# Block 3 of a fused attention and feed-forward kernel in the layout of the other blocks, with another order of units

## The chip, the cores and the metric

The kernel runs on one core of a Trainium2 chip. The metric is the device time of one execution in microseconds (us), the median of several runs. One execution of each kernel is profiled. The profile knows these engines: PE (TensorE, matmuls), PEld (its weight loads), DVE (VectorE), ACT (ScalarE), POOL (GpSimd) and SP (SyncE, which issues DMAs).

## The reference, cut to what matters

```python
xn = layernorm(x)                                   # x: 2048 rows of 640, bf16
q = (xn @ wq).reshape(1, 2048, 32, 192).transpose(0, 2, 1, 3)
k, v = the last 512 rows of each head's cache       # 32 heads, 192 wide
p = softmax(q @ k.T * 192 ** -0.5)
s = (p @ v, heads side by side) @ wo                # 2048 x 640
g = silu((silu(xn @ w_gate) * (xn @ w_up)) @ w_down)  # 2048 x 640
return x + s * g
```

## The kernel before: the parts that matter

The kernel treats the 2048 rows as four blocks of 512, and the 32 heads as 16 pairs. After the feed-forward part (which yields g) come 16 pairs of heads. For each pair and block there are query, score, product (`pv`) and output-projection units; the output projection of every pair is summed in SBUF, the on-chip working memory (`s_m`, `s_t`, `s_o`).

The projection has 640 columns, and no matmul of this kernel writes more than 512. Blocks 0 to 2 split them into 512 row-major columns (`s_m`: rows on partitions) and 128 transposed ones (`s_t`: columns on partitions, all 512 rows of the block in one matmul). Block 3 (`MB`) keeps all 640 row-major, as two halves of 320 (`s_o`). A row tile of a block is 128 of its 512 rows:

```python
HD, MB, MC = D // 2, NB - 1, D - P          # 320, block 3, 512

def wo_units(i):                            # units of one block in a stretch
    ...
    if b == MB:
        return [unit([(qt, cols) for cols in HALVES]) for qt in range(4)]
    return [unit([(2 * h + k, MAIN) for k in range(2)]) for h in range(2)] + [[rest]]
```

A unit's matmuls contract over 64 rows; two of them, on the upper and the lower half of the array, run side by side. In the first turn the two halves write two banks of PSUM (the memory that takes the matmuls' results), in the second turn they change banks. (Where the prediction speaks of row tiles and PSUM banks together, it means these halves of the array.) So that no two row halves ever write one bank together, a tiny GpSimd memset (`turn_t`) waits for the last matmul of the first turn, and the first matmul of the second turn waits for it:

```python
def wo_turn(st, i, tiles, turn):
    ps = st["sc"]
    for j in range(3):
        for n, r in enumerate((lo, hi)):    # rows 0..63, 64..127 of the array
            k = n ^ turn
            qt, cols = tiles[k]
            m = nc.tensor.matmul(
                ps[:, k, 0 : cols.stop - cols.start], OTs[i][r, 3 * qt + j, :],
                pairs[i // NB]["wo"][r, j, cols], ...)
            after(m, st)                    # wait for the memset of the turn before
    if turn == 0:
        turned(m, st)                       # nc.gpsimd.memset(turn_t) after this matmul

def rest():                                 # the transposed 128 columns: a bank for each half
    sc = sc_tile()
    for n, r in enumerate((lo, hi)):
        wo_rest(sc[:, n, :], i, r)
    for n in range(2):
        add_sum(pr + n, s_t[:, b, :], sc[:, n, :])
```

The order in which the units of one pair reach TensorE is written out. A digit is the block, a and b are the two halves of its product, w to z its output-projection units (of the block two earlier), and the last digit is the turn:

```python
LATER = """0a0 0b0 0y0 0x0 0a1 0x1 0w0 0b1 0w1 1x0 1a0 1x1 1b0 1w0 1a1 1w1 1z0 1b1 1z1 1y0 2b0 1y1
    2y0 2b1 2x0 2a0 2x1 3w0 2a1 3w1 2w0 3a0 2w1 3b0 3a1 3y0 3x0 3b1 3x1"""
```

In this text a stretch is one such sequence, about 23.6 us. Thirteen of them, for pairs 1 to 13, run block 3's units. The score and projection units share two PSUM tiles (`sc_tile`), queries and products share two others (`mm_tile`).

The softmax here doesn't subtract the row's maximum and nothing guards it: scores larger than these inputs give would overflow.

Of the kernel before, what the change touches and what calls it, by code (L numbers as in the profile page):

```python
# [15 lines left out]
def kernel(  # L16
# [13 lines left out]
    nc = tc.nc  # L30
# [20 lines left out]
    HD = D // 2  # L51
    MB = NB - 1
# [31 lines left out]
    g_m = res.tile([P, 4 * MB, MC], bf, name="g_m")  # L84
    g_t = res.tile([P, MB, 512], bf, name="g_t")
    g_o = res.tile([P, 4, D], bf, name="g_o")
    xT = res.tile([P, MB, 512], bf, name="xT")

# [82 lines left out]
    with ExitStack() as fctx:  # L171
# [131 lines left out]
        def ffn_down(b, u):  # L303


            dn = mm_tile()[:, 0, :]
            if b == MB:
                ti, n = divmod(u, 2)
                cols = slice(n * HD, (n + 1) * HD)
                dn, to = dn[:, 0:HD], g_o[:, ti, cols]  # L310
            elif u < 4:
                ti, cols = u, slice(0, MC)
                to = g_m[:, 4 * b + u, :]
            else:
                to = g_t[:, b, :]
            for f in range(NF):
                if b < MB and u == 4:
                    at, by = wd_sb[:, f, MC:D], hTs[b][:, f, :]
                else:
                    at, by = hTs[b][:, f, ti * P : (ti + 1) * P], wd_sb[:, f, cols]  # L320
                nc.tensor.matmul(dn, at, by, start=(f == 0), stop=(f == NF - 1))  # L321
            nc.scalar.activation(to, dn, ACT.Silu)
# [66 lines left out]
        for b in range(NB):  # L389
# [4 lines left out]
            for f in range(NF):  # L394
# [13 lines left out]
                if b < MB and f >= 8:  # L408
# [19 lines left out]
        for u in range(8):  # L428
            ffn_down(NB - 1, u)
            if u in (1, 3, 5):  # L430
                q_full(0, u // 2)
# [9 lines left out]
    s_m = sapool.tile([P, 4 * MB, MC], f32, name="s_m")  # L441
    s_t = sapool.tile([P, MB, 512], f32, name="s_t")
    s_o = sapool.tile([P, 4, D], f32, name="s_o")
# [114 lines left out]
    def load_xb(b):  # L558

        xbs[b] = finp.tile([P, 4, D], bf, name="x_b", bufs=NB)  # L560
        n = MC if b < MB else D
        nc.sync.dma_start(
            out=xbs[b][:, :, 0:n],
            in_=x2[b * 512 : (b + 1) * 512, 0:n].rearrange("(t p) d -> p t d", p=P),
        )

    def rows(b, qts):

        if b == MB:
            return s_o[:, qts, :], g_o[:, qts, :]  # L570
# [22 lines left out]
    HALVES = [slice(n * HD, (n + 1) * HD) for n in range(2)]  # L593
# [18 lines left out]
    def wo_turn(st, i, tiles, turn):  # L612

        ps = st["sc"]
        for j in range(3):
            for n, r in enumerate((lo, hi)):
                k = n ^ turn
                qt, cols = tiles[k]
                m = nc.tensor.matmul(  # L619
                    ps[:, k, 0 : cols.stop - cols.start], OTs[i][r, 3 * qt + j, :],  # L620
                    pairs[i // NB]["wo"][r, j, cols],
# [12 lines left out]
    def sum_rows(i, qts, sc):  # L634
        pr, b = divmod(i, NB)
        to, g = rows(b, qts)
        if b == MB:
            to = to.rearrange("p t (n d) -> p (t n) d", n=2)
            sc = sc[:, :, 0:HD]
# [15 lines left out]
    def add_x(b, qts=None):  # L655
        if qts is None:
            to, x = s_t[:, b, :], xT[:, b, :]
        else:
            to, x = rows(b, qts)[0], xbs[b][:, qts, 0 : MC if b < MB else D]
        nc.gpsimd.tensor_tensor(to, to, x, ALU.add)  # L660

    def wo_units(i):
# [4 lines left out]
        def unit(tiles):  # L667
            st, qts = {}, slice(tiles[0][0], tiles[1][0] + 1)

            def first():  # L670
                st["sc"] = sc_tile()
                wo_turn(st, i, tiles, 0)

            def second():
                wo_turn(st, i, tiles, 1)
                sum_rows(i, qts, st["sc"][:, :, :])
# [10 lines left out]
        if b == MB:  # L687
            return [unit([(qt, cols) for cols in HALVES]) for qt in range(4)]
        return [unit([(2 * h + k, MAIN) for k in range(2)]) for h in range(2)] + [[rest]]

    def wo_full(i, q2):

        pr, b = divmod(i, NB)
        if b == MB:
            units = [[(qt, cols) for cols in HALVES] for qt in (2 * q2, 2 * q2 + 1)]
        else:
            units = [[(2 * q2 + k, MAIN) for k in range(2)]]
        for tiles in units:
            sc, qts = sc_tile(), slice(tiles[0][0], tiles[1][0] + 1)
            for k, (qt, cols) in enumerate(tiles):  # L700
                wo_cols(sc[:, k, 0 : cols.stop - cols.start], i, qt, cols)
# [181 lines left out]
```

## Time and profile before

| | kernel before |
|---|---|
| device time, median | 921.71 us (921.47 to 921.82, 3 runs) |
| span of the profiled run | 919.5 us |
| TensorE busy, share of its chain | 99%, 99% |
| VectorE, ScalarE, GpSimd busy | 64%, 52%, 10% |

The prediction below shows the page's shares, the timeline and the last microseconds. What it does not show are the groups of instructions that the change replaces. In this view each line is: source line, engine, operation, out<-in, shapes and count | busy us, mean ns of one | idle time of the engine before them. These are from the view of groups by shape of the kernel before:

```profile
L619 PE MATMUL sc<-wo_p,OT_b 64*128 64x512 bf16 x984 | 128.1, 376 | 0.0
...
L632 DVE TENSOR_TENSOR s_m<-s_m,sc 128x1024 f32<-128x1024 f32 x82 | 100.2, 1222 | 48.7 <-PE sc L619 42.7 <-PE sc L579 5.9
...
L619 PE MATMUL sc<-wo_p,OT_b 64*128 64x320 bf16 x624 | 56.3, 296 | 0.0
L632 DVE TENSOR_TENSOR s_t<-s_t,sc 128x512 f32<-128x512 f32 x82 | 56.2, 685 | 18.0 <-PE sc L587 16.6
...
L632 DVE TENSOR_TENSOR s_o<-s_o,sc 128x640 f32<-128x640 f32 x52 | 42.6, 820 | 16.0 <-PE sc L619 14.8 <-PE sc L579 1.1
```

The 624 matmuls of 320 columns are block 3: 13 stretches of 48. The zero in the last field says that TensorE never sat idle before one of them. A mean of 376 ns for 512 columns is not what a matmul costs in a stream: the matmuls overlap in the pipeline, their ends are modelled, and their starts lie closer. The cost has to be read from start to start in the timeline.

### The profile page before, as it was taken

The numbers are of one execution on the slowest core, as the hardware profiler recorded it, in microseconds if no ns is written. First come the engines' busy times: TensorE is split into PE (matmuls) and PEld (weight loads), VectorE is DVE, ScalarE is ACT, GpSimd is POOL, SyncE is SP. The second block draws the span as 40 slices with busy tenths as digits, with TensorE's granted clock in tenths as the row PEclk, the third lists the DMA queues.
The fourth block names the chain that finished last, engine by engine and source line by source line (L and its number), as shares of the span: only waits on it lengthen the run. The fifth ranks groups of instructions, "written<-read, shape, count | busy, mean of one in ns | idle before, by whom it ended". The sixth has DMA issues, their size and how long they took to land.

```text
span 919.5 us, 23759 instructions
## 1 busy us (share of the span) xinstructions
PE 914.1 (99%) x10193; PEld 565.6 (62%) x10193; DVE 592.2 (64%) x842; ACT 474.3 (52%) x843; POOL 90.2 (10%) x298
## 2 busy tenths in 40 slices
PE   9999999999999999999999999999999999999998
PEld 6444445565757575757575757576666666666665
DVE  6443421467676767777777777676767676767656
ACT  4222222657464646565656555655555555556461
POOL 0000000000000000000000000000000000002977
PEclk9999999999999999999999999999999999999999
DMA  9312520045453425243534353435353434333526
GB/s 311 67 35 63 95 73 1 1 75 113 54 112 53 111 47 112 54 104 59 104 58 109 58 109 57 107 48 101 68 100 58 92 75 80 86 71 108 126 45 169
DMA packets 246969, 77.45 MB, mean 84 GB/s; under 512 B 227792, under 2 KB 246864, under 8 KB 246864
## 3 DMA queue, kind: packets, MB, share of 16 engines
q1 hardware_dynamic: 245376, 74.23, 39.2%
q8 instruction: 80, 1.31, 0.6%
q10 hardware_dynamic: 1488, 1.70, 0.6%
q14 instruction: 25, 0.20, 0.1%
HBM read 39.06 MB, written 2.62 MB: 45 GB/s over the span
## 4 chain that ended last, share of the span: by engine, by line
PE 99%; DVE 0%; POOLq 0%; POOL 0%; issue 0%; ACT 0%; DVEq 0%
PE mm L460 22%; PE sc L474 18%; PE sc L619 16%; PE mm L499 16%; PE sc L282 11%; PE mm L321 6%; PE sc L587 3%; PE sc L579 2%; PE mm L551 2%; PE mm L579 1%; PE gu L230 1%; PE gu L282 0%; PE mm L330 0%; PE sc L551 0%; PE sc L499 0%; PE mm L474 0%
## 5 line engine op out<-in xcount | busy, mean ns | idle before, releaser
L478 ACT ACTIVATE p_t<-sc 128x1024 bf16<-128x1024 f32 x254 | 252.9, 1022 | 120.6 <-PE sc L474 120.6
L465 DVE TENSOR_REDUCE qT<-mm 128x512 bf16<-128x1024 f32 x189 | 231.0, 1222 | 99.2 <-PE mm L460 96.7
L529 ACT ACTIVATE O_b<-mm,r 128x192 bf16<-128x192 f32 x486 | 164.6, 421 | 184.0 <-issue 138.4
L460 PE MATMUL mm<-xnT,wq_p 64*128 64x512 bf16 x1890 | 237.5, 376 | 0.0
L474 PE MATMUL sc<-qT,khat 64*128 64x512 bf16 x1524 | 198.0, 376 | 0.0
L619 PE MATMUL sc<-wo_p,OT_b 64*128 64x512 bf16 (+1 forms) x1608 | 182.1, 345 | 0.0
L499 PE MATMUL mm<-V_p,p_t 64*128 64x193 bf16 x3520 | 181.4, 242 | 0.0
L499 PEld LDWEIGHTS <-p_t 64*128 64x128 bf16 x3584 | 160.9, 93 | 28.8
L460 PEld LDWEIGHTS <-wq_p 64*128 64x128 bf16 x1890 | 105.0, 94 | 98.7 <-issue 0.7
L474 PEld LDWEIGHTS <-khat 64*128 64x128 bf16 x1536 | 85.3, 94 | 80.4 <-DVE s_t L632 0.3
L632 DVE TENSOR_TENSOR s_m<-s_m,sc 128x1024 f32<-128x1024 f32 x82 | 100.2, 1222 | 48.7 <-PE sc L619 42.7
L619 PEld LDWEIGHTS <-OT_b 64*128 64x128 bf16 x1608 | 85.8, 94 | 37.3 <-issue 0.3
L605 POOL MEMSET turn_t<- 128x1 f32 x246 | 24.1, 98 | 698.0 <-PE mm L499 494.7
L290 DVE TENSOR_TENSOR hT<-sc,sg 128x512 bf16<-128x512 f32 x46 | 31.7, 691 | 81.6 <-ACT sg L289 81.6
L632 DVE TENSOR_TENSOR s_t<-s_t,sc 128x512 f32<-128x512 f32 x82 | 56.2, 685 | 18.0 <-PE sc L587 16.6
L289 ACT ACTIVATE sg<-sc 128x512 bf16<-128x512 f32 x46 | 27.3, 596 | 69.8 <-PE sc L282 69.8
L282 PE MATMUL sc<-xnT,wg_sb 128*128 128x512 bf16 (+1 forms) x260 | 60.2, 354 | 0.3 <-ACT xnT L350 0.3
L282 PE MATMUL sc<-xnT,wu_sb 128*128 128x512 bf16 (+1 forms) x260 | 60.2, 354 | 0.0
L632 DVE TENSOR_TENSOR s_o<-s_o,sc 128x640 f32<-128x640 f32 x52 | 42.6, 820 | 16.0 <-PE sc L619 14.8
L321 PE MATMUL mm<-wd_sb,hT 128*128 128x512 bf16 (+1 forms) x240 | 46.7, 347 | 0.0
L518 DVE RECIPROCAL r<-mm 128x4 f32<-128x4 f32 x124 | 22.5, 182 | 37.3 <-PE mm L499 28.4
L282 PEld LDWEIGHTS <-wu_sb 128*128 128x128 bf16 x285 | 27.1, 98 | 27.1 <-issue 0.4
(95 smaller groups left out, 460.8 us busy)
## 6 DMA issues: line engine op xcount, KB each, us to landing
wo_p<-in_A_wo_dram SPq DMA_DIRECT2D x16, 480.0 KB, 4.6
K_p<-in_A_k_cache_dram SPq DMA_DIRECT2D x32, 192.0 KB, 4.3
V_p<-in_A_v_cache_dram SPq DMA_DIRECT2D x32, 192.0 KB, 3.5
wq_p<-in_A_wq_dram SPq DMA_DIRECT2D x64, 80.0 KB, 3.0
wq_p<-in_A_wq_dram SPq DMA_DIRECT2D x16, 160.0 KB, 3.3
x_t<-in_A_x_dram SPq DMA_DIRECT2D x14, 160.0 KB, 3.0
OT_b<-O_b SPq DMA_TRANSPOSE x124, 2.7
wd_sb<-in_B_w_down_dram SPq DMA_DIRECT2D x1, 1920.0 KB, 12.9
```

What stands on the lines that cost most here:

```text
L282: nc.tensor.matmul(out, w_sb[:, c, f * P : (f + 1) * P], xnT[:, c, qc], start=(c == 0), stop=(c == NC - 1),)
L290: nc.vector.tensor_tensor(hTs[b][:, f, :], u, sg[:], ALU.mult)
L321: nc.tensor.matmul(dn, at, by, start=(f == 0), stop=(f == NF - 1))
L460: nc.tensor.matmul(q_ps[:, h, :], pairs[pr]["wq"][r, c, j * P : (j + 1) * P], xnT[r, c, b * 512 : (b + 1) * 512], start=(c == 0), stop=(c ...
L465: nc.vector.reduce_sum(qTs[i][:, j, :], q_ps[:, :, :].rearrange("p h n -> p n h"), axis=AX.X)
L474: nc.tensor.matmul(sc[:, h, :], khat[r, j, ks], qT[r, j, :], start=(j == 0), stop=(j == 2))
L478: nc.scalar.activation(p_t[:, :, :], sc[:, :, :], ACT.Exp, scale=scale)
L499: m = nc.tensor.matmul(acc[:, k, h * 256 : h * 256 + Dh + 1], Ps[i][kc][r, h, qt * P : (qt + 1) * P], V_p[r, kc, h, 0 : Dh + 1], start=(p ...
L529: nc.scalar.activation(O_b[:, qt, h, :], a_k[:, h, 0:Dh], ACT.Copy, scale=r[:, k, h, :])
L579: nc.tensor.matmul(ps, OTs[i][:, 3 * qt + j, :], pairs[i // NB]["wo"][:, j, cols], start=(first and j == 0), stop=(end and j == 2),)
L619: m = nc.tensor.matmul(ps[:, k, 0 : cols.stop - cols.start], OTs[i][r, 3 * qt + j, :], pairs[i // NB]["wo"][r, j, cols], start=(turn == 0 ...
L632: nc.vector.tensor_tensor(to, to, ps, ALU.add)
```

## The change

Block 3 gets the layout of blocks 0 to 2, in the feed-forward part, in the sums and in the tail, and its transposed part is done ahead of its row tiles at the end. The units of a stretch are put in a new order, since block 3 has one unit fewer. The core of the diff:

```diff
-    s_m = sapool.tile([P, 4 * MB, MC], f32, name="s_m")
-    s_t = sapool.tile([P, MB, 512], f32, name="s_t")
-    s_o = sapool.tile([P, 4, D], f32, name="s_o")
+    s_m = sapool.tile([P, T, MC], f32, name="s_m")
+    s_t = sapool.tile([P, NB, 512], f32, name="s_t")
 ...
-        for u in range(8):
+        for u in range(5):
             ffn_down(NB - 1, u)
-            if u in (1, 3, 5):
-                q_full(0, u // 2)
+            if 1 <= u < 4:
+                q_full(0, u - 1)
 ...
-        if b == MB:
-            return [unit([(qt, cols) for cols in HALVES]) for qt in range(4)]
-        return [unit([(2 * h + k, MAIN) for k in range(2)]) for h in range(2)] + [[rest]]
+        return [unit(0), unit(1), [rest]]
 ...
-    LATER = """0a0 0b0 0y0 0x0 0a1 0x1 0w0 0b1 0w1 1x0 1a0 1x1 1b0 1w0 1a1 1w1 1z0 1b1 1z1 1y0 2b0 1y1
-        2y0 2b1 2x0 2a0 2x1 3w0 2a1 3w1 2w0 3a0 2w1 3b0 3a1 3y0 3x0 3b1 3x1"""
+    LATER = """0a0 0b0 0y0 0x0 0a1 0x1 0w0 0b1 0w1 1w0 1b0 1w1 1a0 1b1 1y0 1x0 1a1 1x1 2w0 2a0 2w1
+        2b0 2a1 2y0 2x0 2b1 2x1 3w0 3b0 3w1 3a0 3b1 3y0 3x0 3a1 3x1"""
 ...
     last_rest(2, V, sc_tile)
     last_rows(2, slice(0, 2), G, mm_tile)
-    last_rows(2, slice(2, 3), V, sc_tile)
-    last_rows(2, slice(3, 4), G, mm_tile)
+    last_rest(3, V, sc_tile)
+    last_rows(2, slice(2, 3), V, mm_tile)
+    last_rows(2, slice(3, 4), G, sc_tile)
 ...
-        wo_parts(qt, [(HD, eng, None) for eng in engs])
+        wo_parts(qt, [(eng, None) for eng in engs])
     store(0)
-    wo_parts(3, ((384, G, nc.sync), (D - 384, V, nc.scalar)))
+    wo_parts(3, ((G, nc.sync), (V, nc.scalar)))
```

Left out of this cut: block 0's store moves from SyncE's to ScalarE's queue, and the last part of the last row tile is stored together with its 128 columns of the transposed part (96 KB; the part before it has 64 KB). The intent can be read from it: fewer and wider matmuls, fewer turns, and last row tiles of 512 columns instead of 640, with the other 128 done ahead of them.

More of the change, by code (lines that the diff above doesn't have):

```diff
@@ L50 @@
     PD = 2 * Dh
-    HD = D // 2
-    MB = NB - 1
     MC = D - P
@@ L83 @@
     xnT = res.tile([P, NC, Sq], bf, name="xnT")
-    g_m = res.tile([P, 4 * MB, MC], bf, name="g_m")
-    g_t = res.tile([P, MB, 512], bf, name="g_t")
-    g_o = res.tile([P, 4, D], bf, name="g_o")
-    xT = res.tile([P, MB, 512], bf, name="xT")
+    g_m = res.tile([P, T, MC], bf, name="g_m")
+    g_t = res.tile([P, NB, 512], bf, name="g_t")
+    xT = res.tile([P, NB, 512], bf, name="xT")
     ident = consts.tile([P, P], bf, name="ident")
@@ L306, in ffn_down @@
             dn = mm_tile()[:, 0, :]
-            if b == MB:
-                ti, n = divmod(u, 2)
-                cols = slice(n * HD, (n + 1) * HD)
-                dn, to = dn[:, 0:HD], g_o[:, ti, cols]
-            elif u < 4:
-                ti, cols = u, slice(0, MC)
-                to = g_m[:, 4 * b + u, :]
-            else:
-                to = g_t[:, b, :]
+            to = g_m[:, 4 * b + u, :] if u < 4 else g_t[:, b, :]
             for f in range(NF):
-                if b < MB and u == 4:
+                if u < 4:
+                    at, by = hTs[b][:, f, u * P : (u + 1) * P], wd_sb[:, f, 0:MC]
+                else:
                     at, by = wd_sb[:, f, MC:D], hTs[b][:, f, :]
-                else:
-                    at, by = hTs[b][:, f, ti * P : (ti + 1) * P], wd_sb[:, f, cols]
                 nc.tensor.matmul(dn, at, by, start=(f == 0), stop=(f == NF - 1))
@@ L407 @@
                         ln_transpose_dma(t)
-                if b < MB and f >= 8:
+                if f >= 8:
                     x_transpose(4 * b + f - 8)
@@ L560, in load_xb @@
         xbs[b] = finp.tile([P, 4, D], bf, name="x_b", bufs=NB)
-        n = MC if b < MB else D
         nc.sync.dma_start(
-            out=xbs[b][:, :, 0:n],
-            in_=x2[b * 512 : (b + 1) * 512, 0:n].rearrange("(t p) d -> p t d", p=P),
+            out=xbs[b][:, :, MAIN],
+            in_=x2[b * 512 : (b + 1) * 512, MAIN].rearrange("(t p) d -> p t d", p=P),
         )
     def rows(b, qts):
-        if b == MB:
-            return s_o[:, qts, :], g_o[:, qts, :]
         t = slice(4 * b + qts.start, 4 * b + qts.stop)
@@ L591, in wo_rest @@
             )
-    HALVES = [slice(n * HD, (n + 1) * HD) for n in range(2)]
     MAIN = slice(0, MC)
@@ L610, in after, with wo_turn @@
             follows(m, st.pop("turn"))
-    def wo_turn(st, i, tiles, turn):
+    def wo_turn(st, i, half, turn):
         ps = st["sc"]
@@ L617, in wo_turn @@
                 k = n ^ turn
-                qt, cols = tiles[k]
                 m = nc.tensor.matmul(
-                    ps[:, k, 0 : cols.stop - cols.start], OTs[i][r, 3 * qt + j, :],
-                    pairs[i // NB]["wo"][r, j, cols],
+                    ps[:, k, :], OTs[i][r, 3 * (2 * half + k) + j, :],
+                    pairs[i // NB]["wo"][r, j, MAIN],
                     start=(turn == 0 and j == 0), stop=(turn == 1 and j == 2), skip_group_check=True,
@@ L636, in sum_rows @@
         to, g = rows(b, qts)
-        if b == MB:
-            to = to.rearrange("p t (n d) -> p (t n) d", n=2)
-            sc = sc[:, :, 0:HD]
         if i < 2 and qts.start:
@@ L658, in add_x @@
         else:
-            to, x = rows(b, qts)[0], xbs[b][:, qts, 0 : MC if b < MB else D]
+            to, x = rows(b, qts)[0], xbs[b][:, qts, MAIN]
         nc.gpsimd.tensor_tensor(to, to, x, ALU.add)
@@ L665, in wo_units, with unit @@
         pr, b = divmod(i, NB)
-        def unit(tiles):
-            st, qts = {}, slice(tiles[0][0], tiles[1][0] + 1)
+        def unit(half):
+            st = {}
             def first():
                 st["sc"] = sc_tile()
-                wo_turn(st, i, tiles, 0)
+                wo_turn(st, i, half, 0)
             def second():
-                wo_turn(st, i, tiles, 1)
-                sum_rows(i, qts, st["sc"][:, :, :])
+                wo_turn(st, i, half, 1)
+                sum_rows(i, slice(2 * half, 2 * half + 2), st["sc"][:, :, :])
             return [first, second]
@@ L685, in rest @@
                 add_sum(pr + n, s_t[:, b, :], sc[:, n, :])
-        if b == MB:
-            return [unit([(qt, cols) for cols in HALVES]) for qt in range(4)]
-        return [unit([(2 * h + k, MAIN) for k in range(2)]) for h in range(2)] + [[rest]]
+        return [unit(0), unit(1), [rest]]
     def wo_full(i, q2):
         pr, b = divmod(i, NB)
-        if b == MB:
-            units = [[(qt, cols) for cols in HALVES] for qt in (2 * q2, 2 * q2 + 1)]
-        else:
-            units = [[(2 * q2 + k, MAIN) for k in range(2)]]
-        for tiles in units:
-            sc, qts = sc_tile(), slice(tiles[0][0], tiles[1][0] + 1)
-            for k, (qt, cols) in enumerate(tiles):
-                wo_cols(sc[:, k, 0 : cols.stop - cols.start], i, qt, cols)
-            sum_rows(i, qts, sc[:, :, :])
-            gate(i, qts)
-        if b < MB and q2:
+        sc, qts = sc_tile(), slice(2 * q2, 2 * q2 + 2)
+        for k in range(2):
+            wo_cols(sc[:, k, :], i, 2 * q2 + k, MAIN)
+        sum_rows(i, qts, sc[:, :, :])
+        gate(i, qts)
+        if q2:
             sc = sc_tile()
@@ L743, in wo_parts @@
     def wo_parts(qt, parts):
-        i, t, c0 = NS - 1, 4 * (NB - 1) + qt, 0
-        ob = xbs[MB][:, qt, :]
-        for n, (width, eng, queue) in enumerate(parts):
-            cols, c0 = slice(c0, c0 + width), c0 + width
+        i, b, width = NS - 1, NB - 1, MC // len(parts)
+        t, ob = 4 * b + qt, xbs[b][:, qt, :]
+        for n, (eng, queue) in enumerate(parts):
+            cols = slice(n * width, (n + 1) * width)
             ps = (sc_tile() if n else mm_tile())[:, 0, 0:width]
@@ L752, in wo_parts @@
             wo_cols(ps, i, qt, cols, first=False)
-            finish(ps, ob[:, cols], s_o[:, qt, cols], g_o[:, qt, cols], eng)
+            s, g = rows(b, slice(qt, qt + 1))
+            finish(ps, ob[:, cols], s[:, 0, cols], g[:, 0, cols], eng)
             if queue:
-                queue.dma_start(out=out2[t * P : (t + 1) * P, cols], in_=ob[:, cols])
+                upto = slice(cols.start, D if cols.stop == MC else cols.stop)
+                queue.dma_start(out=out2[t * P : (t + 1) * P, upto], in_=ob[:, upto])
         if not queue:
@@ L783, in stretch @@
             if i >= 2:
-                units.update({"%d%s" % (b, n): u for n, u in zip("wxyz", wo_units(i - 2))})
+                units.update({"%d%s" % (b, n): u for n, u in zip("wxy", wo_units(i - 2))})
         for name in (LATER if pr else FIRST).split():
@@ L835 @@
         if q2:
-            last_rest(b, V if b else G, mm_tile if b else sc_tile)
+            last_rest(b, V, mm_tile if b else sc_tile)
         if more:
             pv_full(i + more[0], more[1])
-        if q2:
-            store_block(b, nc.scalar if b else nc.sync)
+        if b:
+            store_block(q2, nc.scalar)
     last_rest(2, V, sc_tile)
     last_rows(2, slice(0, 2), G, mm_tile)
-    last_rows(2, slice(2, 3), V, sc_tile)
-    last_rows(2, slice(3, 4), G, mm_tile)
+    last_rest(3, V, sc_tile)
+    last_rows(2, slice(2, 3), V, mm_tile)
+    last_rows(2, slice(3, 4), G, sc_tile)
+    store_block(2, nc.scalar)
     for qt, engs in enumerate(((G, V), (G, G), (V, G))):
-        if qt == 1:
-            store_block(2, nc.scalar)
-        elif qt:
+        if qt:
             store(0)
-        wo_parts(qt, [(HD, eng, None) for eng in engs])
+        wo_parts(qt, [(eng, None) for eng in engs])
     store(0)
-    wo_parts(3, ((384, G, nc.sync), (D - 384, V, nc.scalar)))
+    wo_parts(3, ((G, nc.sync), (V, nc.scalar)))
 _INS = ['A_x', 'A_k_cache', 'A_v_cache', 'A_wq', 'A_wo', 'B_x', 'B_w_gate', 'B_w_up', 'B_w_down']
```

## The prediction

> **What bounds the kernel now.** I read the page's busy shares first, then the chain that ended last, then the timeline of TensorE in three places: the end of the feed-forward part, one attention stretch, and the last microseconds. The page:
>
> ```profile
> PE 914.1 (99%) x10193; PEld 565.6 (62%) x10193; DVE 592.2 (64%) x842; ACT 474.3 (52%) x843; POOL 90.2 (10%) x298
> ...
> PE 99%; DVE 0%; POOLq 0%; POOL 0%; issue 0%; ACT 0%; DVEq 0%
> ```
>
> TensorE is busy for 99% of the span and is 99% of the chain. Busy matmuls are pipelined, so this alone does not say that the array streams without holes. The timeline of TensorE does (columns: start, length, engine, line, operation, tiles, shape, count):
>
> ```profile
> 147.84 2.75 PE L321 MATMUL mm<-hT,wd_sb 128*128 128x512 bf16 x12
> 150.43 3.42 PE L321 MATMUL mm<-wd_sb,hT 128*128 128x320 bf16 x24
> 153.69 1.24 PE L330 MATMUL mm<-xnT,wq_p 128*128 128x512 bf16 x5
> ```
>
> From start to start, 12 matmuls of 512 columns take 2.59 us and 24 of 320 columns take 3.26 us. Two equations: (2.59/12 - 3.26/24) us over 192 columns is 0.417 ns per column, a 2.4 GHz column rate, and what remains is about 2.5 ns per matmul. The attention stretch has the same figures for pairs of 64-row matmuls that run side by side:
>
> ```profile
> 284.03 0.85 PE L499 MATMUL mm<-V_p,p_t 64*128 64x193 bf16 x16
> 284.70 0.59 PE L619 MATMUL sc<-wo_p,OT_b 64*128 64x320 bf16 x6
> 285.11 0.85 PE L499 MATMUL mm<-V_p,p_t 64*128 64x193 bf16 x16
> ...
> 290.22 0.83 PE L587 MATMUL sc<-OT_b,wo_p 64*128 64x512 bf16 x6
> 290.87 0.35 PE L499 MATMUL mm<-V_p,p_t 64*128 64x193 bf16 x4
> ```
>
> Six of 320 columns are three pairs: 3 x (133.3 + 2.5) ns = 0.407 us, seen 0.41. Six of 512: 3 x (213.3 + 2.5) = 0.647, seen 0.65. I compared every start in the trace with the one before it plus columns/2.4 + 2.5 ns: over the whole span only 4.8 us are lost, 2.1 of them in the warm-up matmuls at the start and 0.5 at the first transposes. Every stall after 17 us together is some 0.7 us. So the kernel's time is its number of streamed columns, plus 2.5 ns a slot (a slot: a full matmul, or a side-by-side pair), plus the two ends. A wait that ends on another engine costs nothing today.
>
> **What the Trainium skill says.** "TensorE: Matmul & The Clock Gate", section "Back-to-back issue gap", gives N/2.4 + 2.5 ns for a warm stream; the trace agrees (2.59 us for 12 of 512). The same section warns that with a weight load for every matmul the spacing is set by both operations and gives about 81 ns at N=128; here loads of 94 to 98 ns lie beside slots of 136 ns or more, and the spacing shows no sign of them. "TensorEngine Tiling (Array Packing)", section "Gotcha 1: PSUM Pressure", says that row tiles may not use one PSUM bank at once and that software must order them; that is what the 98 ns memset of turn_t does between the two turns of a unit. The transposed part needs no turn, because each row tile has its own bank.
>
> **The change, part by part.** Block 3 used to be 640 row-major columns, in halves of 320. It becomes 512 row-major columns and 128 transposed ones, as blocks 0 to 2 are.
>
> 1. Streamed columns: unchanged. A stretch had 4 row tiles x 2 halves x 3 chunks = 24 pairs of 320 = 7680 columns; it gets 12 pairs of 512 and 3 pairs of 512 = 7680. Feed-forward: 96 x 320 = 60 x 512. Tail (pairs 14 and 15): 48 matmuls, 15,360 columns; then 6 of 512 and 48 of 256, also 15,360.
> 2. Slots: each stretch loses 9 pairs, and pairs 1 to 13 each run one such stretch, so 117. The full-array stage of pair 14 loses 9, the feed-forward 36, and the tail gains 6. Net 156 x 2.5 ns = **0.39 us**, all on the path: 0.29 in the stretches, 0.02, 0.09, and -0.015.
> 3. Weight loads: 18 fewer in a stretch, 94 ns each beside the stream. Worth nothing. So are 26 fewer turn memsets (2 x 13).
> 4. VectorE: four sums of 820 ns become two of 1222 and two of 685 (3.28 to 3.81 us), +0.53 us a stretch. In the stretch of 23.65 us it is busy 15.93 us:
>
> ```profile
> 277.72:301.37 23.65, 23.65 (x396) 18.48 (x394) 15.93 (x27) 11.12 (x31) 1.77 (x18) 1.00 0.33 52
> ```
>
> (fields: window, length, then busy time of PE, weight loads, DVE, ACT, POOL). So 16.5 of 23.6, beside TensorE. In the gate stage GpSimd exchanges 4 x (1402 + 1397) ns for 2 x (2125 + 2125) + 1151 + 1153 = 10.8 us instead of 11.2; it finishes its queue about 6 us before its next task. Nothing.
> 5. DMA: four more 128-column transposes of x in the feed-forward, where the queue is idle. Nothing.
> 6. Order of units. I walked the new order with 0.65 us a unit, a sum 1.22 us, the two transposed sums 1.37, a divide about 1.9 us from PSUM to free, 0.2 us for each hand-over. PSUM has two score tiles and two product tiles. The thinnest spots are the first turn of block 2's unit, three units after block 1's transposed part (about 0.4 us to spare), and block 2's second product three units after block 1's last (0.35). The order before has the same three-unit distance at its start and shows no wait there. At least one unit of 0.65 us stands between the turns of each unit, as before. So 0 expected.
>
> 7. The tail. The lines before:
>
> ```profile
> 914.24 0.48 DVE L721 TENSOR_TENSOR s_f<-sc,g_o 128x320 f32<-128x320 f32 x1
> 914.34 0.65 PE L579 MATMUL mm<-wo_p,OT_b 128*128 128x384 bf16 x3
> ...
> 914.80 1.92 POOL L722 TENSOR_TENSOR x_b<-s_f,s_o 128x320 bf16<-128x320 f32 x2 [0.83 <-DVE s_f L721]
> ...
> 915.68 0.43 DVE L721 TENSOR_TENSOR sc<-sc,g_o 128x256 f32<-128x256 f32 x1
> 916.14 0.42 DVE L722 TENSOR_TENSOR x_b<-sc,s_o 128x256 bf16<-128x256 f32 x1
> 916.60 0.35 ACTq L755 DMA_DIRECT2D out_dram<-x_b  x1
> 916.75 0.33 SPq L755 DMA_DIRECT2D out_dram<-x_b  x1
> ```
>
> The last store waits for GpSimd, which does two additions one after the other (320 and 384 columns, 1.92 us), not for TensorE or for the shorter VectorE half. After: parts of 256 columns, on GpSimd about 0.73 us each (estimate from 860 ns at 320 and 992 at 384), on VectorE 0.43. Walking the engines from the last rows of block 1 (TensorE at 901.84 in the old trace): block 3's transposed part costs 1.38 us of VectorE, but it lies in front of the row tiles; VectorE catches up by the last row tile and starts the last product about 0.2 us after its matmul. In old times TensorE ends at about 915.49, VectorE's last addition at 916.55, GpSimd's at 916.58. Take off the 0.40 us gained earlier: 916.15 and 916.18, so the last stores are issued near 916.2 instead of 916.75. The store of 512 columns is now cut 256 for one queue and 256 + 128 for the other, so the larger one (96 KB, 1.7 us to landing before) is on the ACT queue. End of span about 0.55 us earlier. Moving block 0's store to the ACT queue blocks no ACT work: all divides come before it.
>
> Sum: 0.39 from slots and about 0.17 from the balanced last additions, **0.56 us**. 921.71 - 0.56 = **921.1 us**.
>
> **The rivals.**
> - *A new wait on PSUM in the new order.* For it: VectorE serves the sums in order, and the transposed part's two sums (1.37 us) can push a later reciprocal by 0.3 us where I find 0.35 us to spare. Against: the same distances stand in the order before, without a hole. If 0.1 us is lost in each of 13 stretches: 922.4.
> - *The tail gets worse.* The extra transpose has to land before the row stores, and block 2's store starts about 0.6 us later, next to the last rows' stores. DMA ran at about 350 GB/s from 910 to 915 us before, so a late 640 KB could push the last store by up to 1 us: about 921.9. Against: block 1's store should go earlier, since its transposed part no longer queues behind block 0's store.
> - *Weight loads or VectorE bind somewhere.* Then the gain would be larger: 18 loads of 94 ns x 13 is 22 us of load time (2.4%). Against: the slots of 320 columns last 0.41 us for three, exactly the stream, so no load is waited for. That would be near 900, and I give it next to nothing.
>
> **Range and chances.** The slot term is nearly arithmetic; the tail and the new order carry the doubt. Most of it is on the side of losing the gain, so: 921.1, 8 in 10 between 920.5 and 921.9. A change of 2% is 18 us. No mechanism that I find is a tenth of this: faster 0.01, same 0.98, slower 0.01.
>
> **What would show it right or wrong.** TensorE should still be 99%. The 64x320 group should be gone, and the 64x512 group of the same line should have larger numbers. In the stretch, windows cut at the same units should be about 0.02 us shorter. Group turn_t should count 220 instead of 246. The feed-forward's last downs should end 0.09 us earlier. The last stores should be issued near 916.2 us. If instead a hole appears in TensorE's timeline in each stretch, ended by a sum on VectorE or a divide on ACT, the walk of step 6 was wrong; if TensorE ends near 915.1 but the stores do not follow by 1.1 us, step 7 was.

## The result, and the profile after

| | before | after |
|---|---|---|
| device time, median of 6 runs | 921.80 us (921.47 to 922.14) | 921.04 us (920.74 to 921.94) |
| ratio, 95% interval | | 0.9993 (0.9981 to 1.0006): the same within 2% |
| span of the profiled run | 919.5 us | 919.2 us |

A ratio is the mean time of one kernel's fast runs over that of the other's fast runs of the same rounds, so it is not quite the ratio of the medians. The predicted time was 921.1 us, the forecast was "same", and both held. But the interval includes 1: run times alone do not tell a gain of 0.7 us from none. The traces do, as shown further down. First the page of the changed kernel, its busy shares, its chain and the groups:

```profile
PE 913.1 (99%) x9898; PEld 550.9 (60%) x9920; DVE 601.7 (65%) x844; ACT 474.5 (52%) x840; POOL 85.5 (9%) x269
...
PE 99%; issue 0%; DVE 0%; ACT 0%
...
L614 DVE TENSOR_TENSOR s_m<-s_m,sc 128x1024 f32<-128x1024 f32 x108 | 131.9, 1221 | 60.4 <-PE sc L601 52.3
L601 PE MATMUL sc<-wo_p,OT_b 64*128 64x512 bf16 x1296 | 168.9, 376 | 0.0
...
L614 DVE TENSOR_TENSOR s_t<-s_t,sc 128x512 f32<-128x512 f32 x108 | 74.2, 687 | 28.4 <-PE sc L571 26.6
L588 POOL MEMSET turn_t<- 128x1 f32 x220 | 21.8, 99 | 700.0 <-PE mm L486 506.0
```

The group of 320 columns is gone, its work is in the 1296 matmuls of 512 columns. There are 220 turns (246 before). VectorE went from 592.2 to 601.7 us and nobody noticed: TensorE is still the whole chain. Now the end of the feed-forward part in the timeline of TensorE (start, length, engine, line, operation, tiles, shape, count):

```profile
148.14 2.75 PE L309 MATMUL mm<-hT,wd_sb 128*128 128x512 bf16 x12
150.73 5.34 PE L309 MATMUL mm<-wd_sb,hT 128*128 128x512 bf16 x23
155.91 1.24 PE L318 MATMUL mm<-xnT,wq_p 128*128 128x512 bf16 x5
...
167.01 1.25 PE L447 MATMUL mm<-xnT,wq_p 64*128 64x512 bf16 x10
```

The row of 23 is one of 24; a matmul record is missing from the trace, as a few are. 24 matmuls in 5.18 us (150.73 to 155.91) are again 215.8 ns each. The first row here starts at 148.14; the same matmul of the kernel before started at 147.84. So this execution was 0.30 us behind before any of the changed work had begun. From that row to the first attention matmul it is 18.87 us, against 18.97 before (147.84 to 166.81): 0.10 us won, where 0.09 had been worked out.

The stretch that the prediction showed, in a window cut at the same units:

```profile
277.90:301.53 23.63, 23.63 (x378) 17.54 (x376) 16.59 (x27) 11.15 (x31) 1.59 (x16) 1.00 0.36 52
```

It is 23.63 us (23.65 before), with VectorE at 16.59 instead of 15.93. And the last microseconds of the changed kernel, from the timeline of all engines:

```profile
914.99 1.41 POOL L694 TENSOR_TENSOR x_b<-s_f,s_m 128x256 bf16<-128x256 f32 x2 [0.49 <-DVE s_f L693]
...
915.59 0.43 DVE L693 TENSOR_TENSOR sc<-sc,g_m 128x256 f32<-128x256 f32 x1 [0.16 <-PE sc L563]
916.05 0.42 DVE L694 TENSOR_TENSOR x_b<-sc,s_m 128x256 bf16<-128x256 f32 x1
916.42 0.33 SPq L729 DMA_DIRECT2D out_dram<-x_b  x1
916.51 0.35 ACTq L729 DMA_DIRECT2D out_dram<-x_b  x1
```

GpSimd's last two additions take 1.41 us instead of 1.92 and no longer end last. Less the 0.30 us of the late start, the stores are issued at 916.12 and 916.21; the prediction had 916.2.

**Where the noise sits, and how to count without it.** Two traces of one kernel differ almost only in the first 15 us. The first gate matmul of 512 columns in two traces, the first of the kernel before, the second of a repeat of the changed kernel:

```profile
14.46 1.24 PE L282 MATMUL gu<-xnT,wg_sb 128*128 128x512 bf16 x5
```

```profile
15.40 1.24 PE L279 MATMUL gu<-xnT,wg_sb 128*128 128x512 bf16 x5
```

Over all traces this start lies between 14.46 and 15.63 us, while what follows repeats to 0.02 us in the two traces of each of the two kernels. So I count from it (I call it the mark):

| trace | mark to TensorE's last matmul | last matmul to end of span | mark to end |
|---|---|---|---|
| before | 900.91 | 4.12 | 905.03 |
| before, repeat | 900.91 | 4.13 | 905.04 |
| after | 900.52 | 3.89 | 904.41 |
| after, repeat | 900.52 | 3.91 | 904.43 |

The gain is 0.39 us in the stream and 0.22 us behind it.

### The profile page after: what moved, and what is told of

It is laid out like the page before. It is cut to its first block, busy times and chain, and to the rows that moved or that the text cites. A ratio compares the mean times of both kernels' runs of the same rounds, so it can differ in the third digit from the quotient of the medians.

```text
span 919.2 us, 23149 instructions
## 1 busy us (share of the span) xinstructions
PE 913.1 (99%) x9898; PEld 550.9 (60%) x9920; DVE 601.7 (65%) x844; ACT 474.5 (52%) x840; POOL 85.5 (9%) x269
## 3 DMA queue, kind: packets, MB, share of 16 engines
q8 instruction: 77, 1.26, 0.6%
## 4 chain that ended last, share of the span: by engine, by line
PE 99%; issue 0%; DVE 0%; ACT 0%
PE mm L447 22%; PE sc L461 18%; PE mm L486 16%; PE sc L601 15%; PE sc L279 11%; PE mm L309 6%; PE sc L571 4%; PE sc L563 2%; PE mm L538 2%; PE mm L563 1%; PE gu L227 1%; PE gu L279 0%; PE mm L318 0%; PE sc L486 0%; PE sc L538 0%
## 5 line engine op out<-in xcount | busy, mean ns | idle before, releaser
L486 PE MATMUL mm<-V_p,p_t 64*128 64x193 bf16 x3520 | 176.8, 242 | 0.0
L614 DVE TENSOR_TENSOR s_m<-s_m,sc 128x1024 f32<-128x1024 f32 x108 | 131.9, 1221 | 60.4 <-PE sc L601 52.3
L601 PE MATMUL sc<-wo_p,OT_b 64*128 64x512 bf16 x1296 | 168.9, 376 | 0.0
L601 PEld LDWEIGHTS <-OT_b 64*128 64x128 bf16 x1296 | 70.5, 94 | 43.8 <-issue 0.3
L614 DVE TENSOR_TENSOR s_t<-s_t,sc 128x512 f32<-128x512 f32 x108 | 74.2, 687 | 28.4 <-PE sc L571 26.6
L588 POOL MEMSET turn_t<- 128x1 f32 x220 | 21.8, 99 | 700.0 <-PE mm L486 506.0
L571 PE MATMUL sc<-OT_b,wo_p 64*128 64x512 bf16 (+1 forms) x345 | 50.3, 376 | 0.0
L309 PE MATMUL mm<-wd_sb,hT 128*128 128x512 bf16 x189 | 43.6, 379 | 0.2
L279 PEld LDWEIGHTS <-wg_sb 128*128 128x128 bf16 x285 | 27.2, 98 | 26.4
```

The lines of the kernel that those rows point to most:

```text
L279: nc.tensor.matmul(out, w_sb[:, c, f * P : (f + 1) * P], xnT[:, c, qc], start=(c == 0), stop=(c == NC - 1),)
L309: nc.tensor.matmul(dn, at, by, start=(f == 0), stop=(f == NF - 1))
L486: m = nc.tensor.matmul(acc[:, k, h * 256 : h * 256 + Dh + 1], Ps[i][kc][r, h, qt * P : (qt + 1) * P], V_p[r, kc, h, 0 : Dh + 1], start=(p ...
L571: nc.tensor.matmul(ps.rearrange("p (t q) -> p t q", q=P), pairs[i // NB]["wo"][r, j, MC:D], OTs[i][:, :, :].rearrange("p (t j) q -> p j t ...
L601: m = nc.tensor.matmul(ps[:, k, :], OTs[i][r, 3 * (2 * half + k) + j, :], pairs[i // NB]["wo"][r, j, MAIN], start=(turn == 0 and j == 0), ...
L614: nc.vector.tensor_tensor(to, to, ps, ALU.add)
```

## The experiments

All results were correct, and all timed runs were in the fast state; for a single run the state is unknown, but its trace has a clock of 1.0. Times are medians; the kernel before had 921.74 (9 runs, 921.55 to 921.88) beside the first four kernels and 921.77 (9 runs) beside the next four. "From the mark" is the profiled run, counted as above. Each edit is to the changed kernel.

| run | median us | runs | ratio to before (95%) | from the mark us |
|---|---|---|---|---|
| again | 920.82 | 5 | 0.9993 (0.9979 to 1.0007) | 904.43 |
| old_order | 921.85 | 5 | 1.0003 (0.9990 to 1.0016) | 905.06 |
| halves | 926.63 | 4 | 1.0054 (1.0040 to 1.0068) | 910.32 |
| quarters | 926.86 | 4 | 1.0056 (1.0042 to 1.0069) | 910.38 |
| dve_extra | 938.57 | 4 | 1.0182 (1.0169 to 1.0196) | 921.68 |
| adjacent | 933.12 | 4 | 1.0125 (1.0109 to 1.0140) | 916.28 |
| tail_swap | 921.02 | 5 | 0.9994 (0.9981 to 1.0006) | 904.41 |
| tail_uneven | 922.89 | 1 | one look | 904.81 |
| before_again | 921.81 | 1 | one look | 905.04 |
| old_order_2 | 921.40 | 1 | one look | 904.99 |
| quarters_2 | 927.83 | 1 | one look | 910.69 |

The theory under test: the time is the number of streamed columns, 2.5 ns a slot (a full matmul, or two 64-row matmuls side by side), and the two ends; a wait counts only where the distance between two units is shorter than the release that it waits for. I call it the stream theory. The rivals are named in each expectation.

### again and before_again: is the gain real?

No edit.

> The changed kernel itself, unaltered, once more, to see how well its gain stands clear of the noise. Stream theory (time = streamed columns, plus 2.5 ns a slot, plus the two ends; waits cost only where they reach TensorE): 0.56 us under the kernel before, ratio 0.9994, so about 921.2 where the kernel before has 921.8. Rival (the 0.76 us between the two medians of the first rounds is chance, because single runs of one kernel already differ by 1.2 us): ratio between 0.9998 and 1.0003.

> The kernel before, unaltered, for a second trace of it. Counted from TensorE's first 512-column gate matmul (the stretch ahead of it varied from 14.5 to 15.6 us between traces and carries the noise of single runs), its first trace has 905.03 us to the end of the span, and the changed kernel's two traces 904.41 and 904.43. Stream theory: 905.0 again, within 0.1. Rival (the difference of 0.6 us is itself chance): as far as 0.3 us or more from it.

The medians differ by 0.92 us, and still the interval includes 1, because two of the five runs (921.61 and 922.41) lie 0.8 us and more above the other three. The first of them is the profiled one, and its trace is the one with the late start at 15.40 us; of the other there is no trace. The record lists the core's span for every run, and there the run of 922.41 us has 918.8 us, like the fast ones (918.7 to 918.9): its excess lies outside the span. The nine runs of the kernel before have spans of 919.4 to 919.7 us. The two traces of each kernel agree within 0.02 us from the mark, and the kernels differ by 0.61. So the gain is there; the run times could not show it, the spans suggest it, and two traces of each show it.

### halves and quarters: what a slot costs, and whether weight loads count

```diff
-            for n, r in enumerate((lo, hi)):
-                k = n ^ turn
+            for s, n, r in [(s, n, r) for s in range(2) for n, r in enumerate((lo, hi))]:
+                k, cut = n ^ turn, slice(s * 512 // 2, (s + 1) * 512 // 2)
                 m = nc.tensor.matmul(
-                    ps[:, k, :], OTs[i][r, 3 * (2 * half + k) + j, :],
-                    pairs[i // NB]["wo"][r, j, MAIN],
-                    start=(turn == 0 and j == 0), ...
+                    ps[:, k, cut], OTs[i][r, 3 * (2 * half + k) + j, :],
+                    pairs[i // NB]["wo"][r, j, cut],
+                    start=(turn == 0 and j == 0 and s == 0), ...
```

halves does the same in the query and score units; quarters has 4 for 2, in this unit alone.

> The changed kernel with every 64-row matmul of 512 columns in the query, score and output-projection units of the stretches cut in two of 256 columns on the same weights (each with its own weight load); same columns, right result. It measures the slot term. Stream theory: 945 + 768 + 648 = 2361 more slots of 2.5 ns = +5.9 us, so about 927. Rival (weight loads set the pace of short slots: two loads of 94 ns for a slot of 109 ns, one after the other): far over that, up to 4722 x 79 ns = +370 us. Second rival (the 2.5 ns is not paid for each slot; the gain came from elsewhere): under +1.5 us.

> The changed kernel with only the output-projection units of the stretches cut in four of 128 columns on the same weights; same columns, right result. Slots go from 648 to 2592, each of 55.8 ns by the stream rule, which is less than the 94 ns that the trace shows for one weight load. Stream theory: 1944 x 2.5 ns = +4.9 us, so about 926. Rival (below some width the weight load sets the pace): [...]with 94 ns +99 us. The timeline of TensorE shows the slot's length directly.

halves is 5.81 us over again in its median, and 5.90 from the mark (910.32 less 904.42). Worked out: 5.9. quarters is 6.04 over in its median and 5.96 from the mark, 1.1 more than 4.9. The timeline of TensorE in quarters shows the slots:

```profile
281.73 1.52 PE L601 MATMUL sc<-wo_p,OT_b 64*128 64x128 bf16 x48
283.06 0.85 PE L486 MATMUL mm<-V_p,p_t 64*128 64x193 bf16 x16
```

48 matmuls are 24 slots, from 281.73 to 283.06: 55.4 ns each, 128/2.4 + 2.5 = 55.8 worked out. Two weight loads of 94 ns go with each slot and are not felt. So the load rival is out down to 128 columns. The trace of the kernel before had already answered it: near the start, 20 full-array matmuls of 128 columns in the first gate and up projections (w_gate, w_up), each with its own load, start between 8.82 and 9.88 us: 19 distances of 55.8 ns. Where is the rest? In one hole near the end, in the groups of quarters by shape:

```profile
L563 PE MATMUL sc<-wo_p,OT_b 128*128 128x512 bf16 x75 | 18.3, 379 | 0.9 <-DMA OT_b<-O_b 0.9
```

From start to start that hole is 1.10 us: the first row tile of the last pair waits for the DMA transpose of its input. To see whether it belongs to the short matmuls I ran the same kernel again.

> The kernel cut in four of 128 columns once more. Its first trace had a single hole of 1.1 us near the end, ended by a late landing of a transpose, beside 4.9 us from slots. Theory: the hole is chance and the slots are not: counted from the first 512-column gate matmul 4.9 us over the changed kernel's 904.4, or that plus one hole that the timeline shows. Rival (short matmuls bring that hole about): the hole at the same place again.

From the mark it is 6.27 us over the changed kernel, with a hole of 1.39 us at the same place. 6.27 - 1.39 = 4.88 and 5.96 - 1.10 = 4.86: the slots cost 4.9 us as worked out, and the hole comes back, so my theory of chance was wrong and the rival's forecast came true. What it may come from is told after the next experiment.

### old_order, old_order_2: what the new order is for

```diff
-    LATER = """... 0w1 1w0 1b0 1w1 1a0 1b1 1y0 1x0 1a1 1x1 2w0 2a0 2w1
-        2b0 2a1 2y0 2x0 2b1 2x1 3w0 3b0 3w1 3a0 3b1 3y0 3x0 3a1 3x1"""
+    LATER = """... 0w1 1x0 1a0 1x1 1b0 1w0 1a1 1w1 1b1 1y0 2b0
+        2y0 2b1 2x0 2a0 2x1 3w0 2a1 3w1 2w0 3a0 2w1 3b0 3a1 3y0 3x0 3b1 3x1"""
```

> The new layout of block 3 with the order of units of before, its fourth unit struck out. It asks what the new order is for. Stream theory: the first product of block 2 now stands three units (1.97 us) behind the second half of the product whose PSUM tile it takes (it was five units), while the divide needs about 1.98 us from the product's end until the tile is free: a hole of 0 to 0.15 us in each of 13 stretches, 0 to +2 us over the changed kernel, seen in TensorE's timeline as a hole in front of the first product of block 2. Rival (the order is worth a clear part of the gain by itself, for instance through fewer waits in every stretch): more than +2 us.

The median is 1.03 us over again, and from the mark it is 0.64 over. The size was in the expected range, the cause was not: there is no hole in front of block 2's product. TensorE has two holes of 0.26 and 0.39 us, in 2 of 13 stretches, in front of unit 3w0. The prediction's walk had looked at PSUM tiles alone; this unit waits for a DMA.

> The new layout in the old order once more. Its first trace had two holes, 0.26 and 0.39 us, in 2 of 13 stretches, and not in front of block 2's product as expected, but in front of block 3's first unit, ended by the landing of the transpose of block 1's output. Theory: that unit stands only 5.9 us behind the end of the product that it needs (6.6 in the changed kernel, 6.7 before), so late landings of a 2.7 us transpose show here and not there: again some holes at this place in a few stretches, of 0.1 to 1 us, none elsewhere. Rival (one unlucky execution): no hole.

The repeat has the two holes in the same two stretches, 0.29 and 0.28 us. The timeline of the repeat, second of the two:

```profile
574.83 1.75 PE L601 MATMUL sc<-wo_p,OT_b 64*128 64x512 bf16 x12
...
575.75 0.33 PEld L601 LDWEIGHTS <-OT_b 64*128 64x128 bf16 x6 [0.61 <-DMA OT_b<-O_b]
```

The row of 12 takes in 2x1 and 3w0; without the hole, 12 matmuls last 1.47 us in this timeline. The weight loads of 3w0 wait for the landing of block 1's transposed output. From the end of the product 1a1 to 3w0 the old order has nine units in the new layout, 5.9 us (0.65 us a projection unit, 0.67 a product unit); in the changed kernel it is ten, 6.6 us; in the kernel before it was 6.7 us, with five of its twelve units only 0.41 us long. That is what the new order gives back. Both traces of the old order are at 904.99 and 905.06 from the mark, and the kernel before is at 905.03: two holes of 0.3 us would have eaten the whole gain of the layout.

**Why in just those stretches, and why in quarters.** In each trace I sorted the 124 transposes of the attention part by whether a packet of the DMA queues that the page calls instruction started between issue and landing. In the changed kernel, 76 had none: median 2.75 us from issue to landing, at most 3.6. 48 had one: median 3.8 us, at most 4.65. A longer transpose has more time to meet a packet, but counting only packets in the first 2.7 us after issue gives the same 76 and 48. The other traces agree (in the kernel before two transposes went above 3.8 us without one, one in each of its two traces). The two transposes behind the holes of old_order took 4.2 and 4.3 us and had such packets. quarters has more instructions, and 133 of these packets on its page instead of 102; one falls on the first transpose of the last pair, which there takes 4.3 us (4.6 in quarters_2) instead of 2.8 and has a matmul waiting. This is a coincidence in time found in all traces; no run moved those packets on purpose, so the cause is argued, not shown.

### dve_extra: does VectorE's average share tell whether it has room?

```diff
             for n in range(2):
                 add_sum(pr + n, s_t[:, b, :], sc[:, n, :])
+            nc.vector.tensor_tensor(sc[:, 1, :], sc[:, 1, :], g_t[:, b, :], ALU.mult)
```

> The changed kernel with one more VectorE operation of about 0.69 us on the score tile after each transposed part in the stretches (it multiplies PSUM that nobody reads afterwards; right result). VectorE's share of a stretch goes from about 16.5 to 19.3 of 23.6 us, still under the span. Stream theory with the walk of distances: a transposed part's tile is taken again three units later (1.96 us), and it is free after 0.2 + 1.37 + 0.69 = 2.26 us, so a hole of about 0.35 us at three places in each of 13 stretches: +14 us (10 to 20). Rival (what counts is the average share: VectorE has room for all of it): within 1 us of the changed kernel.

It is 17.75 us over again in the median and 17.3 from the mark. By the sum of its work VectorE would be idle for a sixth of each stretch or more (16.6 + 4 x 0.69 of 23.6 us), and the kernel still loses 1.9% against the changed one. The waits of this run (engine and tile, line, releaser: us in total, times, longest):

```profile
PE sc L601 <- DVE r L505: 6.6, 26, 0.3
...
PE sc L601 <- DVE sc L665: 2.0, 13, 0.2
```

26 and 13 are three holes in each of 13 stretches, at the three places named in advance. (The profile names the VectorE operation that ended last before the start, a reciprocal in two of the three.) This view counts from modelled ends and so shows less than is lost. From start to start the three holes are 0.34, 0.42 and 0.42 us, where 0.35 was expected, and a fourth of 0.08 at the stretch's end had not been foreseen: 13 x 1.26 = 16.4, and 0.8 in the first stretch. So the walk of distances is right to about 0.1 us, and on the optimistic side.

### adjacent: what a turn costs when nothing hides it

```diff
-    ... 0w1 1w0 1b0 1w1 1a0 1b1 1y0 1x0 1a1 1x1 2w0 ...
+    ... 0w1 1b0 1w0 1w1 1a0 1b1 1y0 1a1 1x0 1x1 2w0 ...
```

> The changed kernel with the two turns of each of block 3's row units one right after the other, the unit that stood between them put in front. Same work. Stream theory: TensorE then waits for the drain of its last matmul (163 ns longer than its stream), GpSimd's memset of 98 ns and two hand-overs of about 45 ns, in all about 0.35 us for each of 26 turns: +9 us (5 to 12). Rival (a turn costs next to nothing, or costs the same hidden or not, and the 26 turns that the change saved are part of its gain): within 1.5 us of the changed kernel.

It is 12.3 us over again in the median, 11.86 from the mark. The timeline:

```profile
285.43 0.81 PE L601 MATMUL sc<-wo_p,OT_b 64*128 64x512 bf16 x6
...
286.37 0.10 POOL L588 MEMSET turn_t<- 128x1 f32 x1 [0.55 <-PE sc L601]
286.52 0.33 PEld L601 LDWEIGHTS <-OT_b 64*128 64x128 bf16 x6 [0.77 <-POOL turn_t L588]
286.52 0.82 PE L601 MATMUL sc<-wo_p,OT_b 64*128 64x512 bf16 x6 [0.28 <-POOL turn_t L588]
```

The first turn's six matmuls are streamed by 286.08 (285.43 + 0.647), the memset starts 0.29 us later, and the second turn starts at 286.52: a hole of 0.445 us, 26 times, 11.6 us. I had worked out 0.35, with 45 ns for each hand-over. From the modelled end of the matmul to the memset the traces have 0.13 us (median 0.12 over the 246 turns of the kernel before), from the memset to the next matmul 0.06: 0.163 + 0.127 + 0.098 + 0.057 = 0.445. Hidden behind one unit of 0.65 us it costs nothing: the changed kernel and the kernel before have no TensorE wait on it at all, so the 26 turns that the change saves are no part of its gain.

### tail_swap and tail_uneven: what sets the end

```diff
+            k = len(parts) - 1 - n if queue else n          # tail_swap
-            cols = slice(n * width, (n + 1) * width)
+            cols = slice(k * width, (k + 1) * width)
```

```diff
             cols = slice(n * width, (n + 1) * width)
+            if queue:                                       # tail_uneven
+                cols = (slice(0, 384), slice(384, MC))[n]
```

> The changed kernel with the last row tile's two column parts swapped, so that the part stored together with the transposed columns (96 KB) is the one finished first, and the last store has 64 KB. Theory: 64 KB landed 1.6 us after issue and 96 KB 1.75 us, so the last landing is about 0.1 us earlier: 0.1 us less than the changed kernel, which only the trace can show. Rival (the landing does not depend on the size at this scale): no change in the trace either.

> The changed kernel with its last row tile cut 384 (GpSimd) and 128 (VectorE) instead of 256 and 256, nearer to the cut of the kernel before. Theory of the prediction's last step (the GpSimd addition of the last part, not TensorE, sets the last store): GpSimd's last addition is 0.27 us longer and starts up to 0.15 us later, so the store behind it is issued 0.25 to 0.45 us later than in the changed kernel, counted from TensorE's last matmul. Rival (the stores wait for TensorE's end): no change.

tail_swap changes nothing: its last store, now 64 KB, landed 1.75 us after its issue, the 96 KB store in its place 1.76 us (in again 1.77). The rival was right for the end: in the last place the landing does not follow the bytes. In the place before it a little is seen, 1.64 us for 96 KB here against 1.56 for 64 KB in the changed kernel. tail_uneven is 0.39 us longer from the mark (904.81 against 904.42). Its last lines:

```profile
915.70 0.56 DVE L693 TENSOR_TENSOR s_f<-mm,g_m 128x384 f32<-128x384 f32 x1 [0.41 <-PE mm L563]
916.17 0.29 DVE L693 TENSOR_TENSOR sc<-sc,g_m 128x128 f32<-128x128 f32 x1
916.33 0.99 POOL L694 TENSOR_TENSOR x_b<-s_f,s_m 128x384 bf16<-128x384 f32 x1 [0.24 <-DVE s_f L693]
916.49 0.29 DVE L694 TENSOR_TENSOR x_b<-sc,s_m 128x128 bf16<-128x128 f32 x1
916.82 0.35 ACTq L731 DMA_DIRECT2D out_dram<-x_b  x1
917.35 0.33 SPq L731 DMA_DIRECT2D out_dram<-x_b  x1
```

TensorE's last matmul starts at 915.70 here, so the last store is issued 1.65 us after it, against 1.23 in the changed kernel: 0.42 us, inside the expected range. GpSimd's 0.99 us for 384 columns, behind VectorE's 0.56, is what the end waits for. TensorE's last matmul is at the same place within 0.06 us of the mark; the stores follow GpSimd.

No run points to a kernel that is faster than the changed one: tail_swap, 921.02 us, is not to be told from it.

## Why the prediction was right, point by point

- **Streamed columns unchanged, 156 slots fewer, 0.39 us (steps 1 and 2).** Right to the hundredth: mark to last matmul went from 900.91 to 900.52 in two traces of each. Its price of 2.5 ns a slot was tested at 15 times the size in halves (5.90 us for 2361 slots) and at 12 times in quarters (4.9 for 1944).
- **Weight loads and turns are worth nothing (step 3).** Right. The argument used for the loads was weaker than it could have been: it set loads of 94 ns against slots of 136 ns. The trace of before already had product slots of 83 ns with two loads each and full-array slots of 55.8 ns near its start, and quarters goes to 55 ns.
- **VectorE +0.53 us a stretch, beside the stream (step 4).** It was 0.66, and beside the stream. But dve_extra shows how thin this was: another 0.69 us after each transposed part would have cost 17 us. The share of 16.5 in 23.6 us that the step quotes was no reason; the distances of step 6 were.
- **No new wait in the new order (step 6).** Right: the changed kernel's TensorE has no hole in any stretch with block 3's units. The walk was incomplete all the same. It followed PSUM tiles and not the transposed output in SBUF, and that is where the old order breaks in the new layout. That the new order leaves 6.6 us there, enough for the late landings, was not weighed: this part was luck. The rival "a new wait on PSUM" did not come about.
- **The tail, 0.17 us (step 7).** The measured part behind the last matmul is 0.22 us. 0.15 is the earlier issue of the last store, counted from TensorE's last matmul (1.38 to 1.23 us); that is the step's mechanism, confirmed by tail_uneven. The 96 KB landed in 1.76 instead of 1.73 us. The remaining 0.11 us came after the landing: the closing sequence took 0.90 instead of 1.01 us, which nobody had predicted. It goes with the queue of the store that lands last: 0.90 to 0.91 us in the ten traces where that is ScalarE's, 0.97 to 1.01 in the three (before, before_again, tail_uneven) where it is SyncE's. No run changed the queue alone, so the cause stays open; this half of the measured 0.22 us was luck.
- **The sum.** 0.39 + 0.22 = 0.61 us by the traces, 0.56 predicted; without the 0.11 that nobody foresaw it would have been 0.50. The medians of the first rounds differ by 0.76.
- **The rival "the tail gets worse"** did not happen: block 2's store was issued at 912.48 (911.49 before), but block 1's at 907.05 (909.18), as argued (each in its own trace; 0.30 us is the late start).

## What to carry to other kernels

When the timeline shows TensorE streaming without holes, count columns and slots: in this kernel's stream a relayout of the same columns was worth 2.5 ns for each slot saved, and no more, however many loads and turns it removed. What it does to the end comes on top and is read from the last microseconds (here 0.22 us of 0.61). In such a kernel the order of units is what keeps other engines' work free, and it must be checked for each buffer and each transfer that a unit waits for, DMA landings with their late cases included; average shares say nothing about it. For effects under 0.1% compare traces from a mark behind the noisy start, with two traces of each kernel.

## What the Trainium skill lacked or had wrong

- "TensorE: Matmul & The Clock Gate", section "Back-to-back issue gap", gives about 131 ns a matmul at N=512 and about 81 ns at N=128 as sustained spacing of a stream of load and matmul pairs, and calls N/2.4 + 2.5 ns the isolated gap. Here streams with a load for each matmul keep N/2.4 + 2.5: 215.8 ns at 512 columns and 55.8 at 128 for full-array matmuls, 109 at 256 and 55.4 at 128 for pairs of 64-row matmuls side by side, with two loads a slot. The same page's section "Wait — 56ns, not 53.3ns?" gives this spacing for back-to-back matmuls (215.7 ns at N=512), so it is the first section that is off.
- "TensorEngine Tiling (Array Packing)", section "Key Properties", says that changing the tiling mode drains TensorE and gives no time. Each of the four changes between 128-row and 64-row matmuls in the traces left a hole of 94 to 113 ns.
- The same page, section "Gotcha 1: PSUM Pressure", asks software to order row tiles that share a bank and gives no price. Here an order through another engine cost 0.445 us when nothing stood between, and nothing behind a unit of 0.65 us.
- "DMA: Bandwidth & Descriptors", section "DMA Transpose (X-bar)", has no time for a transpose, and "VectorE: DVE Perf Modes", section "The three transpose paths", has one for 128 x 128 only (1309 ns). Here the transposes of 128 x 768 bf16 landed 2.75 us after issue (median), and 3.8 us (at most 4.65) when a packet of the instruction queues started meanwhile. No page connects the two.
